# Stacked score operands built by the compute engines instead of by transfers, and products with v moved from five to seven tiles behind their scores

## The chip, the cores and the metric

The kernel runs on one core of a Trainium2 chip. A core has five engines with a queue each, which run their instructions in order: TensorE (PE; its weight loads are listed as PEld), VectorE (DVE), ScalarE (ACT), GpSimd (POOL) and SyncE (SP), which here only starts transfers. Sixteen DMA engines carry the transfers. SBUF is the memory on the core, with 128 partitions; PSUM takes TensorE's results. The metric is the time of one execution on the device in microseconds, as the median of several runs.

## The reference

Four batches of eight attention heads, 768 positions, 64 features a head; then a gating network of 512 model features and 1024 hidden features. Keys and queries are hashed to six bits each, and a query attends to the keys of its own bucket only:

```python
q_bits = (np.einsum('bhsd,dk->bhsk', q, proj) > 0).astype(np.int64)
k_bits = (np.einsum('bhsd,dk->bhsk', k, proj) > 0).astype(np.int64)
q_bucket = np.sum(q_bits * powers, axis=-1)
k_bucket = np.sum(k_bits * powers, axis=-1)
mask = q_bucket[:, :, :, None] == k_bucket[:, :, None, :]
scores = np.where(mask, scale * np.matmul(q, k.transpose(0, 1, 3, 2)), -1000000000.0)
scores = scores - np.max(scores, axis=-1, keepdims=True)
attn = np.exp(scores)
attn = attn / (np.sum(attn, axis=-1, keepdims=True) + 1e-09)
return np.matmul(attn, v).astype(np.float32)

h = np.maximum(x @ w_in, 0.0)      # x: the heads side by side
u, v = (h[..., :d_ff // 2], h[..., d_ff // 2:])
v_n = (v - mu) / np.sqrt(var + 1e-06)
v_s = np.einsum('ts,bsd->btd', w_spatial, v_n) + b_spatial[None, :, None]
gated = u * v_s
return (gated @ w_out).astype(np.float32)
```

## The kernel before, in words

The 32 heads are taken in 16 pairs, one pair on 128 partitions (64 features of each of two heads). Everything is computed in halves of 16 bits: a value is a rounded f16 (the high half) plus an f16 remainder (the low half).

*Loading and splitting a pair.* `load_qk` fetches k and q of a pair. `hash_rows` multiplies them with the projection on TensorE and makes the signs, `sg`, on VectorE: four strips of 32 partitions, one for each half of the 768 positions of k and of q (L178), then scaled in a second instruction (L180). `split_qk` makes the tile `hl` with four planes of 768: plane 1 and 2 are the high halves of k and q (ScalarE, L186), plane 0 and 3 the low halves of q and of k (VectorE, L187 and L188).

*Stacking a head.* `build(n)` fills one of four tiles `ab` of 128 x 4 x 768. Two matmuls per half then give a tile of scores with mask: one over 128 partitions, which adds high by low and low by high, and one that adds high by high and the hash codes, which stand under the 64 features and push a pair of different buckets far down. `build` works with transfers: the codes by four small ones per head (`ab<-sg`, L203), the low halves by a large one (`ab<-hl`, L216 or L217), and for the heads 8 to 31 (`near`) the upper planes by two copies on VectorE (L209, L210). For odd heads from 8 on the stack is upside down, so that the copies stay on their partitions. The small transfers start from SP's queue for heads 0 to 7 and from ScalarE's queue for the rest. `build(n + 2)` runs while head n is worked on.

*Scores.* Heads 1 to 7 (`KEYS`) are worked key-major: `row_max` first finds the maxima, then `scores_k` gives exponentials that are used as weights of `weighted_k` without a transpose. Head 0 and heads 8 to 31 are query-major, six tiles of 128 queries each: `scores` does two times two matmuls (L300, L301) into one of two PSUM tiles, VectorE evicts them with the row maximum (L302), ScalarE makes the exponential (L304) and its high half (L307), VectorE or GpSimd the low half (L308), and SP starts a transpose of both halves (L310, `pt<-pp`, 128 x 1536 f16). `weighted` multiplies the transposed tile with v in 18 matmuls (L323 to L325). There are six buffers for `pt`, four for `pp` and four for `ex`.

*The gating network.* After every eighth head 28 units of it are queued and mixed between the tiles: `vps` (L372), `ups` (L413), `sps` (L428), `ops` (L443). Those of the last batch have nothing left to be mixed with.

*What sets the order.* The loop at the end of the kernel runs over g, the number of a tile; `at(g, k)` gives the instructions a priority, and a scheduler fixes each engine's order when the program is built. `weighted` of tile t is emitted at step t + `LAG`, `LAG` being 5. `tc.issue_after(x)` keeps instructions behind x in their engine's order.

## Time and profile before

| what | value |
|---|---|
| median of 3 runs | 709.54 us (708.9 to 712.29) |
| the profiled execution | 708.95 us |
| its span, first to last instruction | 707.2 us |
| granted TensorE clock, mean | 0.964 |
| busy: TensorE, VectorE, ScalarE, GpSimd | 618.5, 511.3, 454.2, 222.0 us |
| TensorE's weight loads | 391.0 us |
| transfers: of SP's and ScalarE's queues | 109.67 MB, 77.0% of 16 engines' span |
| `pt<-pp` transposes, `ab<-hl`, `ab<-sg` | 150, 41, 128 transfers |

Busy shares are means over stretches that differ: a start in which the first operands are made, the key-major heads, the query-major heads with the gating network between them, and an end with the gating network alone. In rows of waits the engine that waits stands first and what ended its wait behind the arrow. In rows of groups the shape of the result stands ahead of `<-`, then the count, the busy time, the mean of one in ns, and the idle time before them. The clock is a share of full speed.

### The profile page before, as it was taken

How to read it: one execution, taken by the hardware profiler on the slowest of the kernel's cores; microseconds unless marked ns; L12 is line 12 of the kernel's file. 1: busy time of each engine (PE TensorE's matmuls, PEld its weight loads, DVE VectorE, ACT ScalarE, POOL GpSimd, SP SyncE). 2: the span in 40 equal slices, each digit the busy share in tenths (PEclk: the TensorE clock that was granted, in tenths of full speed). 3: DMA queues.
4: the chain of work that ended last, by engine and by line, in shares of the span. 5: the costliest groups of instructions: out<-in, count | busy, mean ns of one | idle time of the engine just before them, and what ended most of it. 6: DMA issues, size and time to landing. Idle time of an engine off the chain costs nothing.

```text
span 707.2 us, 14858 instructions
## 1 busy us (share of the span) xinstructions
PE 618.5 (87%) x5735; PEld 391.0 (55%) x5735; DVE 511.3 (72%) x961; ACT 454.2 (64%) x806; POOL 222.0 (31%) x215
## 2 busy tenths in 40 slices
PE   1668798999796989999796999899888999999997
PEld 0236676778453655565454565565445655655553
DVE  4665698388888897779699897899697987725100
ACT  1444477567686868777588786868677688724121
POOL 5111434454324452152002162033022530322513
PEclk9999798699899999999998999999999999999999
DMA  9557557353698979998989999999989899950011
GB/s 242 143 109 185 125 154 161 89 163 106 134 185 176 184 161 199 217 194 192 206 153 214 165 197 191 201 185 215 214 171 151 158 180 206 156 132 1 0 45 45
DMA packets 286555, 111.51 MB, mean 158 GB/s; under 512 B 270356, under 2 KB 273428, under 8 KB 286484
## 3 DMA queue, kind: packets, MB, share of 16 engines
q1 hardware_dynamic: 284180, 109.67, 77.0%
q10 hardware_dynamic: 2304, 0.89, 0.6%
q8 instruction: 45, 0.74, 0.4%
q14 instruction: 26, 0.21, 0.1%
HBM read 28.33 MB, written 6.29 MB: 49 GB/s over the span
## 4 chain that ended last, share of the span: by engine, by line
PE 48%; DMA 22%; DVE 11%; issue 7%; SPq 4%; ACT 4%; POOL 4%; ACTq 0%; DVEq 0%; POOLq 0%
DMA pt<-pp 14%; PE sps L428 7%; PE ops L443 7%; PE vps L372 6%; PE ups L413 6%; PE pv L282 4%; DMA ab<-hl 4%; PE sp L300 3%; PE sp L301 3%; PE pv L323 3%; SPq L310 2%; PE pv L325 2%; PE pv L324 2%; DVE ex L302 2%; PE sp L269 1%
## 5 line engine op out<-in xcount | busy, mean ns | idle before, releaser
L302 DVE TENSOR_SCALAR_CACHE_REDUCE ex<-sp 128x768 f32<-128x768 f32 x150 | 141.8, 951 | 42.1 <-PE sp L301 39.7
L304 ACT ACTIVATE ex<-ex,nb 128x768 f32<-128x768 f32 x150 | 139.3, 932 | 7.4 <-ACT nb L303 4.5
L323 PE MATMUL pv<-vp,pt 128*128 128x65 f16 x900 | 105.7, 196 | 43.3 <-DMA pt<-pp 42.7
L307 ACT CAST pp<-ex 128x768 f16<-128x768 f32 x150 | 123.7, 826 | 10.5 <-DMA pt<-pp 5.2
L308 DVE TENSOR_TENSOR pp<-ex,pp 128x768 f16<-128x768 f32 x116 | 123.1, 1064 | 9.5 <-ACT pp L307 8.9
L308 POOL TENSOR_TENSOR pp<-ex,pp 128x768 f16<-128x768 f32 x34 | 57.9, 1702 | 218.0 <-ACT pp L307 175.3
L323 PEld LDWEIGHTS <-pt 128*128 128x128 f16 x900 | 85.5, 100 | 70.7 <-DMA pt<-pp 61.8
L300 PE MATMUL sp<-ab 128*128 128x384 f16 x300 | 102.1, 340 | 14.4 <-DMA ab<-hl 9.3
L324 PE MATMUL pv<-vp,pt 128*128 128x64 f16 x900 | 105.4, 196 | 0.0
L325 PE MATMUL pv<-vp,pt 128*128 128x65 f16 x900 | 104.8, 197 | 0.0
L301 PE MATMUL sp<-ab 127*128 127x384 f16 (+1 forms) x300 | 102.2, 341 | 0.6 <-DMA ab<-sg 0.6
L428 PE MATMUL sps<-ws,vn 128*128 128x384 f16 x576 | 100.7, 326 | 0.5 <-DVE sy L432 0.5
L324 PEld LDWEIGHTS <-pt 128*128 128x128 f16 x900 | 85.9, 99 | 10.7 <-issue 1.9
L325 PEld LDWEIGHTS <-pt 128*128 128x128 f16 x900 | 86.0, 99 | 2.3 <-issue 0.6
L428 PEld LDWEIGHTS <-vn 128*128 128x128 f16 x576 | 54.3, 98 | 35.1 <-issue 1.8
L282 PEld LDWEIGHTS pv<-vf,ex 128*128 128x128 f32 x504 | 69.2, 210 | 3.2 <-issue 1.0
L372 PE MATMUL vps<-wi,xt 128*128 128x512 f16 x288 | 67.4, 382 | 3.2 <-DMA xt<-xs 3.2
L413 PE MATMUL ups<-xt,wi 128*128 128x384 f16 x384 | 69.4, 333 | 0.0
L443 PE MATMUL ops<-wo,g 128*128 128x512 f16 x288 | 67.8, 379 | 1.0 <-ACT o L447 0.9
L282 PE MATMUL pv<-vf,ex 128*128 128x65 f32 x504 | 68.0, 289 | 0.0
L303 ACT ACTIVATE nb<-mx 128x1 f32<-128x1 f32 x150 | 29.3, 197 | 57.2 <-DVE ex L302 56.2
L433 POOL TENSOR_TENSOR sy<-sy,u 128x384 f32<-128x384 f32 x32 | 35.9, 1125 | 75.5 <-DVE sy L432 54.5
(91 smaller groups left out, 920.8 us busy)
## 6 DMA issues: line engine op xcount, KB each, us to landing
qk<-kq SPq DMA_DIRECT2D x16, 768.0 KB
ab<-hl SPq DMA_DIRECT2D x34, 192.0 KB
out<-o SPq DMA_DIRECT2D x24, 256.0 KB
v<-v SPq DMA_DIRECT2D x13, 384.0 KB
raw<-w_in SPq DMA_DIRECT2D x16, 256.0 KB
ab<-hl SPq DMA_DIRECT2D x7, 384.0 KB
pt<-pp SPq DMA_TRANSPOSE x150
raw<-w_sp SPq DMA_DIRECT2D x12, 192.0 KB
```

What stands on the lines that cost most here:

```text
L282: nc.tensor.matmul(acc[:, qi, :], lhsT=ex[:, qi * P:(qi + 1) * P], rhs=vf[p % 2][:, 2 * i + e, :], start=(i == 0 and qi == 0), stop=(i == ...
L300: nc.tensor.matmul(ps[:, c], lhsT=t[:, 0, qs], rhs=t[:, 1, cs], start=True, stop=False)
L301: nc.tensor.matmul(ps[:, c], lhsT=t[0:K, 3, qs], rhs=t[0:K, 2, cs], start=False, stop=True)
L302: nc.vector.tensor_scalar(ex, ps, -float(2 ** 28), None, op0=ALU.max, op1=ALU.max, accum_out=mx)
L304: st["ex", n, i] = nc.scalar.activation(ex, ex, AF.Exp, bias=nb, scale=ISQ).ins
L307: nc.scalar.copy(pp[:, 0], ex)
L308: (nc.gpsimd if i in (PL_POOL if n >= 2 * NH else PL_POOL1) else nc.vector).tensor_tensor(out=pp[:, 1], in0=ex, in1=pp[:, 0], op=ALU.subtract)
L323: nc.tensor.matmul(acc, lhsT=pt[:, c, :], rhs=vh, start=(i == 0 and c == 0), stop=False)
L324: nc.tensor.matmul(acc[:, 0:D], lhsT=pt[:, c, :], rhs=vl, start=False, stop=False)
L325: nc.tensor.matmul(acc, lhsT=pt[:, NT + c, :], rhs=vh, start=False, stop=(i == NT - 1 and c == NT - 1))
L428: nc.tensor.matmul(ps[:, :HS], lhsT=vn[gv][:, c, d * P:(d + 1) * P], rhs=ws[gw][:, c, hs], start=(k == 0), stop=(k == 3 * NT - 1))
L443: nc.tensor.matmul(ps, lhsT=gt[h][gg][:, c, j * P:(j + 1) * P], rhs=wo[gw][:, c, :], start=(k == 0), stop=(k == 3 * NF - 1))
```

## The change

All transfers of `build` go. `build(n)` returns four parts, each an instruction or a few on an engine:

- `codes`: for each of the four strips one instruction that multiplies `sg` of 32 partitions with a column of a mask `hm` and writes 32 x 384 under the features; two on ScalarE and two on VectorE (all four on ScalarE for head 0). The mask holds the scale where the strip belongs to this head and zero elsewhere, so that L180 goes too. It is made once at the start by GpSimd and two instructions on VectorE.
- `high`: a copy of 64 x 1536, on GpSimd for even heads and VectorE for odd ones (ScalarE for head 0).
- `low`: a copy of 64 x 1536 on VectorE.
- `cross`: a copy of 64 x 1536 to the lower partitions, on VectorE for even heads and GpSimd for odd ones.

All heads now have the features on top, the clears of L199 go, and the second matmul uses 127 partitions for every head. For heads 8 to 31 the four parts are issued in four steps instead of one. `LAG` becomes 7. The half-precision copy, the low half and the transpose of a tile leave `scores` and become `halves`, called one step of the loop later with the same priority as before. `split_v` and `load_v` move by a few steps to match, and the row maxima of head 1 are spread over the first four steps.

```diff
+    hm = const.tile([P, 2], F32, name="hm")
+    hw = const.tile([P, 2, 4], F32, name="hw")
+    nc.gpsimd.memset(hw, 1.0)
+    nc.gpsimd.affine_select(out=hw, in_=hw, compare_op=ALU.is_ge, fill=0.0, base=0,
+                            pattern=[[-16, 2], [-32, 4]], channel_multiplier=1)
...
-        s1 = wk.tile([P, HS], F16, tag="sg1", bufs=2, name=f"sg1_{p}")
-        nc.vector.tensor_scalar(s1, s0, hv[:, 1:2], None, op0=ALU.mult)
-        st["sg", p] = s1
+        st["sg", p] = s0
...
-        q_s, q_h = (BQ_S[n >= NH], BQ_H[n >= NH])
-        near = n >= NH
-        z = D - D * e if near else D
-        if near and e and n < NH + NAB:
-            nc.gpsimd.memset(t[0:D, 2:4, :], 0.0)
-        if n < 1:
-            nc.sync.dma_start(out=t[0:D, 2:4], in_=hl[r, 1:3])
-        for j in range(4):
-            q_s.dma_start(
-                out=t[z:z + 2 * NB, 3 - j // 2, (j % 2) * HS:(j % 2 + 1) * HS],
-                in_=sg[32 * j + 16 * e:32 * j + 16 * e + 2 * NB, :])
-        if n < 1:
-            q_h.dma_start(out=t[0:D, 0:2], in_=hl[r, 0:2])
-        elif near:
-            nc.vector.tensor_copy(t[r, 2:4], hl[r, 1:3])
-            nc.vector.tensor_copy(t[r, 0:2], hl[r, 0:2])
-        else:
-
-            top = hl[r, 0:2]
-            (ps, pn), (ss, sn), (es, en) = top.ap
-            src = replace(top, ap=[(ps, pn), (ss, 2), (ss, 2), (es, en)])
-            q_h.dma_start(out=t[0:D].rearrange("p (a b) s -> p a b s", b=2), in_=src)
-        q_h.dma_start(out=t[z:z + D, 0:2], in_=hl[r, 2:4])
+
+        def codes():
+            for j in range(4):
+                js, hs = slice(32 * j, 32 * j + 32), slice((j % 2) * HS, (j % 2 + 1) * HS)
+                to = t[D:D + 32, 3 - j // 2, hs]
+                if j < 2 or n == 0:
+                    st["code"] = nc.scalar.activation(to, sg[js], AF.Copy, scale=hm[js, e:e + 1]).ins
+                else:
+                    nc.vector.tensor_scalar(to, sg[js], hm[js, e:e + 1], None, op0=ALU.mult)
+
+        def high():
+            if n == 0:
+                nc.scalar.copy(t[0:D, 2:4], hl[r, 1:3])
+            else:
+                OWN[e].tensor_copy(t[0:D, 2:4], hl[r, 1:3])
+
+        def low():
+            nc.vector.tensor_copy(t[0:D, 0:2], hl[r, 0:2])
+
+        def cross():
+            eng = nc.vector if n == 0 else OWN[1 - e]
+            st["cross"] = eng.tensor_copy(t[D:P, 0:2], hl[r, 2:4]).ins
+
+        return [codes, high, low, cross]
+
+    OWN = (nc.gpsimd, nc.vector)
...
-        K = P if n % 2 and n >= NH else P - 1
+        K = P - 1
...
-        at(NT * n + i + G_H, 50)
+        st["e32", n, i] = ex
+
+    def halves(n, i):
+        ex = st.pop(("e32", n, i))
...
-    LAG = 5
+    LAG = 7
+    SPL = 1
...
-            if i == BI and n + 2 < N:
-                build(n + 2)
+            if i == 0 and n + 2 < N:
+                parts = build(n + 2)
+            for part in parts[:1] if n + 2 >= NH else parts:
+                part()
+                parts = parts[1:]
...
+        if 0 <= g - SPL < N * NT and (g - SPL) // NT not in KEYS:
+            at(g - SPL + G_H, 50)
+            halves(*divmod(g - SPL, NT))
```

How the change moves instructions is seen at three places. In the rows a tile's own number stands ahead of the number of its buffer.

TensorE, where the products of tile 0 of head 21 begin (`ab_83` before and `ab_88` now are head 21, `ab_89` is head 22; the middle number of `sp_` and `pt_` is the tile). Before:

```order
L300 MATMUL sp_5_5594<-ab_83 128x384
L301 LDWEIGHTS ab_83
L301 MATMUL sp_5_5594<-ab_83 128x384
L323 LDWEIGHTS pt_0_5368
L323 MATMUL pv_5609<-vp_94,pt_0_5368 128x65
```

and now:

```order
L308 MATMUL sp_1_5611<-ab_89 128x384
L309 LDWEIGHTS ab_89
L309 MATMUL sp_1_5611<-ab_89 128x384
L334 LDWEIGHTS pt_0_5335
L334 MATMUL pv_5625<-vp_99,pt_0_5335 128x65
```

Before, the last scores ahead of the first product were those of tile 5 of the same head, five tiles on; now they are those of tile 1 of the next head, seven tiles on. Behind the last product with v of head 31 stand 18 matmuls of the third batch's network before, and 54 now.

VectorE, where the heads 26 and 27 (pair 13) are stacked while head 23's tiles are evicted. Before:

```order
L187 SCALAR_TENSOR_TENSOR hl_6063<-qk_5607,hl_6063 128x768
L188 SCALAR_TENSOR_TENSOR hl_6063<-qk_5607,hl_6063 128x768
L209 COPY ab_84<-hl_6063 64x1536
L209 COPY ab_85<-hl_6063 64x1536
L332 RECIPROCAL rv_6141<-rv_6141 128x6
L210 COPY ab_84<-hl_6063 64x1536
L210 COPY ab_85<-hl_6063 64x1536
```

and now:

```order
L192 SCALAR_TENSOR_TENSOR hl_5977<-qk_5508,hl_5977 128x768
L193 SCALAR_TENSOR_TENSOR hl_5977<-qk_5508,hl_5977 128x768
L208 TENSOR_SCALAR ab_90<-sg_13_5940,hm 32x384
L310 TENSOR_SCALAR ex_5_6060,mx_5817<-sp_5_6061 128x768
L208 TENSOR_SCALAR ab_90<-sg_13_5940,hm 32x384
L214 COPY ab_90<-hl_5977 64x1536
L319 TENSOR_TENSOR pp_3_6037<-ex_3_5967,pp_3_6037 128x768
L217 COPY ab_89<-hl_5977 64x1536
L217 COPY ab_90<-hl_5977 64x1536
L221 COPY ab_89<-hl_5977 64x1536
```

The four copies stay four; two of VectorE's four code writes of the pair come between (the other two stand a few rows earlier), and an eviction and a subtraction now stand among them.

ScalarE at the start of the program. Before:

```order
L186 ACTIVATE hl_121<-qk_110 128x1536
L223 ACTIVATE vp_94<-v_0_140 128x12x64
L186 ACTIVATE hl_167<-qk_132 128x1536
L303 ACTIVATE nb_142<-mx_143 128x1
L304 ACTIVATE ex_0_144<-ex_0_144,nb_142 128x768
```

and now:

```order
L191 ACTIVATE hl_126<-qk_115 128x1536
L212 COPY ab_87<-hl_126 64x1536
L206 ACTIVATE ab_87<-sg_0_124,hm 32x384 x4
L206 ACTIVATE ab_88<-sg_0_124,hm 32x384 x2
L231 ACTIVATE vp_99<-v_0_137 128x12x64
L311 ACTIVATE nb_148<-mx_149 128x1
L312 ACTIVATE ex_0_150<-ex_0_150,nb_148 128x768
```

The stacking of head 0 and half the codes of head 1 stand ahead of the first exponential, and the split of the second pair comes behind it.

More of the change, by code (lines that the diff above doesn't have):

```diff
@@ L176, in hash_rows @@
                 start=True, stop=True, tile_position=(0, 32 * j))
[L177 removed]
+        s0 = wk.tile([P, HS], F16, tag="sg0", bufs=2, name=f"sg0_{p}")
         nc.vector.tensor_scalar(s0, hp[:, :HS], 0.0, hv[:, 0:1], op0=ALU.is_gt, op1=ALU.subtract)
[L179 to L181 removed]
+        st["sg", p] = s0
     def split_qk(p):
@@ L501, in lsh_attention_spatial_gating @@
     load_qk(0)
+    nc.vector.reduce_sum(hm, hw, axis=AX.X)
+    nc.vector.tensor_scalar(hm, hm, hv[:, 1:2], None, op0=ALU.mult)
     hash_rows(0)
+    at(-40, 1)
     split_qk(0)
-    build(0)
-    load_qk(1)
-    build(1)
-    load_v(0)
+    at(-39, 0)
+    for part in build(0):
+        part()
+    load_v(0)
+    at(-38, 0)
+    load_qk(1)
+    at(0, 150)
+    first = st["cross"], st["code"]
+    with tc.issue_after(first[0]), tc.issue_after(first[1]):
+        for part in build(1):
+            part()
     at(-1, 0)
@@ L513, in lsh_attention_spatial_gating @@
     wv = 0
-    rml = [(NT * n + i - NT - LEAD, n, i) for n in sorted(KEYS) for i in range(NT)]
+    rml = [((0, 1, 2, 2, 3, 3)[i] if n == 1 else NT * n + i - NT - LEAD, n, i) for n in sorted(KEYS) for i in range(NT)]
     for g in range(N * NT + LAG):
@@ L524, in lsh_attention_spatial_gating @@
                 split_qk(1)
-                split_v(0)
+                with tc.issue_after(first[0]), tc.issue_after(first[1]):
+                    split_v(0)
                 load_qk(2)
@@ L534, in lsh_attention_spatial_gating @@
             stack = ExitStack()
-            if n not in KEYS:
+            if n not in KEYS and 'tr' in st:
                 stack.enter_context(tc.issue_after(st["tr"]))
-            if BQ_S[n + 2 >= NH] is nc.scalar or BQ_H[n + 2 >= NH] is nc.scalar:
+            if n + 2 >= NH:
                 stack.enter_context(tc.issue_after(st["ex", n, i]))
-            if i == BI and n + 2 < N:
-                build(n + 2)
+            if i == 0 and n + 2 < N:
+                parts = build(n + 2)
+            for part in parts[:1] if n + 2 >= NH else parts:
+                part()
+                parts = parts[1:]
             if n % 2 == 0:
```

12 lines of the change are left out of this document (6 added, 6 removed).

## The prediction

> **What bounds the kernel now.** I read the page first, then the span by stretches, then the chain and the waits of the longest stretch, then single groups and a stretch of the timeline. The page's span and its chain of waits by engine:
>
> ```profile
> span 707.2 us, 14858 instructions
> PE 48%; DMA 22%; DVE 11%; issue 7%; SPq 4%; ACT 4%; POOL 4%; ACTq 0%; DVEq 0%; POOLq 0%
> ```
>
> The execution took 708.95 us, of which 707.2 are the span; the median of the three runs shown is 709.54, 0.6 more. The chain is half TensorE, a fifth DMA. By stretches (the columns after the bounds are length, busy us of PE, PEld, DVE, ACT and POOL, granted clock, DMA share, GB/s):
>
> ```profile
> core 0: us, PE busy (x) PEld busy (x) DVE busy (x) ACT busy (x) POOL busy (x), PEclk, DMA share, GB/s
> 0.00:40.00 40.00, 16.97 (x69) 6.29 (x69) 21.32 (x29) 12.38 (x15) 13.61 (x25) 1.00 0.80 191
> 40.00:80.00 40.00, 27.74 (x247) 20.18 (x248) 27.03 (x54) 19.28 (x36) 7.67 (x10) 0.99 0.65 154
> 80.00:180.00 100.00, 96.27 (x661) 77.42 (x660) 75.52 (x155) 64.78 (x128) 45.01 (x59) 0.87 0.47 127
> 180.00:625.00 445.00, 400.16 (x4332) 246.47 (x4331) 372.23 (x688) 336.97 (x589) 133.72 (x100) 0.97 0.99 185
> 625.00:707.00 82.00, 77.39 (x431) 40.64 (x429) 15.18 (x38) 20.80 (x42) 22.00 (x22) 1.00 0.10 34
> ```
>
> The last 82 us are the gating network of the last batch, TensorE alone; nothing there is touched. From 80 to 180 us TensorE is busy 96 of 100. The stretch from 180 to 625 is where the query-major heads 8 to 31 run: TensorE 400 of 445, VectorE 372, ScalarE 337, DMA share 0.99. Nobody is full, so a loop of waits must set the pace. Its chain and its waits:
>
> ```profile
> by line: DMA pt<-pp 20.9%; issue 7.6%; PE ops L443 6.4%; PE sps L428 5.9%; PE ups L413 5.9%; PE vps L372 5.5%; PE sp L300 5.0%; PE sp L301 4.8%; PE pv L323 3.9%; DMA ab<-hl 3.5%; PE pv L325 3.2%; PE pv L324 3.1%; SPq L310 2.9%; DVE ex L302
> ACT nb L303 <- DVE ex L302: 40.3, 37, 3.8
> DVE ex L302 <- PE sp L301: 37.8, 33, 3.4
> PE pv L323 <- DMA pt<-pp: 36.6, 32, 3.2
> PEld L323 <- DMA pt<-pp: 53.6, 47, 3.6
> SPq L310 <- PE pv L325: 54.9, 40, 3.2
> ```
>
> The transposes lead the chain with 20.9% (93 us). TensorE waits 36.6 us for them at the first product with v of a tile; VectorE then waits 37.8 us for scores that stand behind that product in TensorE's order, and ScalarE 40.3 us for VectorE. The three numbers are one stall, passed on.
>
> **The change part by part.**
>
> *A, the distance of seven.* Products now stand seven tiles behind their scores instead of five (rows of TensorE ahead). A tile takes about 445/143 = 3.1 us here, so a transpose gets some 6 us more before it is asked for. I take all of the 36.6 us away from TensorE; bounds: nothing, and 53.6 us (the wait of the weight load, which contains it). What comes late next is VectorE, so the gain is counted there. Its idle time in the stretch is 445 - 372.2 = 72.8 us; without the 37.8 behind scores, 35 us stay.
>
> *B, VectorE's and GpSimd's new work in that stretch.* The rows:
>
> ```profile
> L180 DVE TENSOR_SCALAR sg<-sg,hc 128x384 f16<-128x384 f16 x10 | 6.8, 684 | 0.1
> L180 DVE TENSOR_SCALAR sg<-sg,hc x16: 301/318/1781, 11.1 to 546.4; 128x384 f16<-128x384 f16 x16
> L209 DVE COPY ab<-hl x24: 540/554/1420, 127.6 to 551.0; 64x1536 f16<-64x1536 f16 x24
> L85 DVE MEMSET ab<- 64x768 uint32 x2 | 1.4, 698 | 1.1 <-PEq L618 1.0
> L86 DVE MEMSET ab<- 32x768 f16 x2 | 1.4, 698 | 0.3 <-DVE ab L85 0.2
> L85 POOL MEMSET ab<- 64x1536 f16 x2 | 2.7, 1376 | 0.1
> L308 POOL TENSOR_TENSOR pp<-ex,pp x34: 1634/1647/2453, 26.7 to 612.5; 128x768 f16<-128x768 f32 x34
> ```
>
> Per pair of heads VectorE had four copies of 64x1536 and the second scaling of the codes (L180); now it has four copies of that shape again (one high, two low, one cross) and four code writes of 32x384, and GpSimd has two copies. A clear of 64 partitions and one of 32 both took 698 ns, so a code write of 32x384 is priced like L180's 128x384: median 318 ns. That is 4 x 0.318 - 0.318 = 0.95 us a pair, 9.5 us over the ten pairs of the stretch. With the stretch's mean of 684 ns, which holds waits, it is 20.5. I take 10, because the waits are priced apart: GpSimd. A GpSimd copy of 64x1536 is not in the trace; below it stands the clear of that size, 1.38 us, above it two of L308's subtractions of 768 elements, 2 x 1.65 = 3.3 us. Twenty copies are 28 to 66 us on an engine that is busy 134 of 445, so GpSimd itself bears them. What they cost VectorE:
>
> ```profile
> L308 DVE TENSOR_TENSOR pp<-ex,pp x116: 916/954/2398, 33.2 to 619.8; 128x768 f16<-128x768 f32 x116
> L308 DVE TENSOR_TENSOR pp<-ex,pp 128x768 f16<-128x768 f32 x112 | 118.7, 1062 | 8.3 <-ACT pp L307 7.7
> L302 DVE TENSOR_SCALAR_CACHE_REDUCE ex<-sp x150: 910/952/960, 23.6 to 615.9; 128x768 f32<-128x768 f32 x150
> 549.90 5.36 POOL L401 TENSOR_TENSOR vn<-vr,vn 128x512 f16<-128x512 f32 x3 [5.71 <-ACT vn L400]
> 550.44 1.98 DVE L209 COPY ab<-hl 64x1536 f16<-64x1536 f16 x2
> 552.45 1.80 DVE L308 TENSOR_TENSOR pp<-ex,pp 128x768 f16<-128x768 f32 x1
> ```
>
> Next to GpSimd's three operations the two copies took 1.98 us instead of 1.11 and a pair of operands out of SBUF 1.80 instead of 0.95, while the eviction from PSUM never passes 0.96. L308 loses (1062 - 954) x 112 = 12 us and L180 (684 - 318) x 10 = 4 us to 134 us of GpSimd, 0.12 us per us; for 28 to 66 us of copies that is 3 to 8 us, at most all 66. I take 4. Together VectorE has 372 + 14 busy and 35 idle: 421 instead of 445, a gain of **24 us**.
>
> *ScalarE* gets two code writes a head. The nearest row is a cast of 128x384:
>
> ```profile
> L434 ACT CAST g<-sy 128x384 f16<-128x384 f32 x32 | 16.3, 509 | 38.9 <-POOL sy L433 37.4 <-DMA ab<-sg 1.4
> L203 ACTq DMA_DIRECT2D ab<-sg x96: 727/736/1569, 149.9 to 574.1; - x96
> L217 SPq DMA_DIRECT2D ab<-hl x32: 462/865/1644, 10.0 to 578.9; - x32
> ```
>
> 20 heads x 2 x 0.51 = 20 us on an engine that is busy 337 of 445 and idles 40 of it behind VectorE; hidden there, and 20 us if that cover went. In exchange ScalarE's queue loses 96 issues of 0.74 us, SP's the issue of 0.87 us that stood between transposes once a head. The four clears of GpSimd and the two table instructions that make the masks run while the first load is under way. The removed bytes, (192 + 36) KB a head or 4.6 MB of the stretch's 185 GB/s x 445 us = 82 MB, also make room for the transposes. No separate gain is booked.
>
> *C, the start.* The first heads were stacked by transfers alone:
>
> ```profile
> 5.61 1.48 ACT L186 ACTIVATE hl<-qk 128x1536 f16<-128x1536 f32 x1 [3.60 <-DMA qk<-kq]
> 8.57 1.20 DVE L188 SCALAR_TENSOR_TENSOR hl<-qk,hl 128x768 f16<-128x768 f32 x1
> 16.49 0.50 PE L300 MATMUL sp<-ab 128*128 128x384 f16 x1 [9.27 <-DMA ab<-hl]
> 20.60 0.48 PE L301 MATMUL sp<-ab 127*128 127x384 f16 x1 [0.61 <-DMA ab<-sg]
> 23.62 0.95 DVE L302 TENSOR_SCALAR_CACHE_REDUCE ex<-sp 128x768 f32<-128x768 f32 x1
> ```
>
> q and k are split at 9.8 us, the scores begin whole only at 20.60. Now VectorE does the codes (0.61) and two copies (2 x 0.55) after 9.8 and is done at 11.5; ScalarE writes four codes of 0.5 after 10.4 and is done at 12.4. That is 8 us earlier. Head 1's stacking and the second pair's split now stand in VectorE's order between the first evictions, so I book **-7** (0 to -10).
>
> *D, to 180 us.* Pairs 1 to 3 now cost VectorE four copies and the codes: 4 x 0.55 + 0.95 = 3.2 us each, pairs 4 and 5 0.95, together 11.4 us in 140 us of which it was busy 103. TensorE sets that stretch (96 of 100): **+2** (0 to +11).
>
> *E, the end.* In TensorE's new order 54 matmuls of the third batch's network stand behind the last product with v, before 18.
>
> ```profile
> 418.02 5.85 PE sps L428 x36
> ```
>
> 36 of them took 5.85 us. They cost that if TensorE does not set the stretch before, nothing if it does; **+3**.
>
> Sum: 708.95 - 24 - 7 + 2 + 3 = 683 in the profile's own time, 683.5 as a median of runs: **683**.
>
> **The rivals.**
>
> *R1, the six buffers hold.* Only six transposed tiles fit, so the transpose of tile t must wait for the products of tile t - 6, which now stand a tile later than the scores of t. SP already waits 54.9 us, 40 times, for exactly that release. Against it: from that release to its own product a tile still has five others, about 15 us, and the longest single piece of a transpose on the chain is
>
> ```profile
> 406.45 6.69 DMA pt<-pp
> ```
>
> If half the stall stays, VectorE idles 35 + 19 = 54: 372 + 14 + 54 = 440, a gain of 5; 708.95 - 5 - 2 + 0.6 = **703**.
>
> *R2, slower: GpSimd's copies stop VectorE.* Each new copy runs where VectorE is to start one of its own. If each costs VectorE 2.3 us (the middle of 1.38 and 3.3), 20 are 46: 372 + 10 + 46 + 35 = 463, 18 more than now; with the other terms 708.95 + 18 - 2 + 0.6 = **726**. It decides once a copy costs more than (37.8 - 10)/20 = 1.4 us. The trace has 0.12 us per us, against it; the 550 us rows, where single instructions lose 0.85, are for it. The Trainium skill (SBUF — State Buffer, "Who interferes with whom") says that a VectorE instruction in a two-port mode or with two inputs in SBUF and a GpSimd instruction exclude one another for the whole instruction, whoever issued first; the rows at 550 us and the steady 0.96 us of the PSUM eviction agree with it. By that rule taken at its worst the time would be the 726 above; the mean of 0.12 says that most instructions miss each other.
>
> *R3, more is gained.* If the idle 35 us halve as well, 372 + 14 + 18 = 404, just above TensorE's 400: -41, and the time is 708.95 - 41 - 2 + 0.6 = **666**. For it: the 40 us of ScalarE's wait have the same root.
>
> That the DMA engines were the bound (share 0.99) would hardly move the time from the forecast: 4.6 of 82 MB is 5.5% of 445, 25 us. The change would then work by its bytes, not by its distance, and only experiments tell the two apart.
>
> **How the numbers follow.** The forecast has 0.58 (its own range 672 to 695, from VectorE's 9.5 to 20.5 us and the bounds of C, D and E), R1 0.17, R2 0.13, R3 0.12. The range reaches into R3 and over R1 to where R2 begins: 660 to 712. A measurement of this kernel tells about 0.5%, 3.5 us, from no change. Faster: 0.58 + 0.12 + 0.10 of R1 = 0.80; the rest of R1 is no change, 0.07; R2 0.13.
>
> **What would show it.** Right: in the stretch of the query-major heads TensorE's wait for transposes under 10 us instead of 36.6, VectorE's wait for scores under 15, VectorE busy 93% or so; first eviction near 13 us; 32x384 code writes near 0.3 us. R1: SP's wait for the products above 100 us and TensorE's wait still near 18. R2: L308's successor on VectorE well above 1.06 us on the mean, copies above 1 us. R3: VectorE above 95%. Wrong altogether: a code write or a GpSimd copy several times dearer than its nearest row, or TensorE's clock granted well below 0.97 there.

## The result, and the profile after

The changed kernel takes **742.1 us** (median of four executions, three of which took 739.48 to 742.69) against 709.56 of the kernel before beside it: a ratio of 1.0439, 95% interval 1.0395 to 1.0483. It is slower by 31 us by the ratio and 33 by the medians, where 683 was forecast and 712 was the upper end of the range. The fourth execution took 1027.49 us at about half the TensorE clock from end to end; the medians here and below count such slow executions, the ratios and intervals do not. The profile shown here is of another execution of the same kernel, 739.81 us. A second series of the same kernel gave 740.62 us, ratio 1.0476 (1.0408 to 1.0544).

The page of the changed kernel, span and busy time of the engines:

```profile
span 737.8 us, 14773 instructions
PE 626.9 (85%) x5735; PEld 396.7 (54%) x5735; DVE 589.8 (80%) x1025; ACT 493.7 (67%) x873; POOL 282.9 (38%) x247
```

VectorE was busy 511.3 us before and is now busy 78.5 us longer. By stretches, cut at 180 us and near the end of the query-major heads (625 us before and 655 now):

```profile
core 0: us, PE busy (x) PEld busy (x) DVE busy (x) ACT busy (x) POOL busy (x), PEclk, DMA share, GB/s
0.00:40.00 40.00, 16.04 (x109) 6.90 (x110) 34.91 (x48) 21.78 (x29) 19.64 (x30) 0.87 0.54 138
40.00:80.00 40.00, 34.26 (x224) 25.18 (x224) 32.58 (x61) 21.63 (x39) 12.98 (x17) 0.73 0.43 113
80.00:180.00 100.00, 89.15 (x661) 69.69 (x660) 79.69 (x149) 65.22 (x124) 48.59 (x56) 0.96 0.35 103
180.00:655.00 475.00, 409.95 (x4329) 254.47 (x4328) 428.73 (x736) 364.19 (x640) 177.86 (x124) 0.94 0.88 164
655.00:738.00 83.00, 77.53 (x417) 40.42 (x414) 13.86 (x34) 20.89 (x42) 23.84 (x24) 1.00 0.10 33
```

The loss lies in one row: the query-major stretch takes 475 us instead of 445, 30 of the 30.6 us by which the span grew. These cuts are times, and the two programs are not quite at the same place there. Cut by the program instead, the part from the first eviction of head 8 to the last product with v takes 478.6 us instead of 449.3, 29.3 more; head 8 begins 5.8 us earlier (172.48 us against 178.26), and what stands behind the last product takes 7.1 us longer (86.72 us against 79.62). In the long stretch VectorE is now the busiest engine, 428.7 us instead of 372.2, and the granted clock is 0.94 instead of 0.97. Its waits:

```profile
ACT nb L311 <- DVE ex L310: 74.9, 38, 7.3
PE sp L308 <- DVE ex L310: 40.3, 23, 3.9
PEld L334 <- DMA pt<-pp: 17.6, 16, 3.7
PE pv L334 <- DMA pt<-pp: 13.1, 13, 3.2
DVE ex L310 <- PE sp L309: 7.0, 10, 2.6
```

The direction of the stall has turned round. TensorE's wait for transposes fell from 36.6 to 13.1 us and VectorE's wait for scores from 37.8 to 7.0, as step A said. But TensorE now waits 40.3 us until VectorE has evicted a score tile, and ScalarE 74.9 us for VectorE (40.3 before). VectorE is late. Before, TensorE's wait for an eviction in the stretch was:

```profile
PE sp L300 <- DVE ex L302: 3.8, 7, 0.9
```

Why it is late is in the groups of instructions by shape (mean of one in ns behind the busy time):

```profile
L319 DVE TENSOR_TENSOR pp<-ex,pp 128x768 f16<-128x768 f32 x116 | 123.6, 1069 | 18.5 <-ACT pp L318 18.0
L208 DVE TENSOR_SCALAR ab<-sg,hm 32x384 f16<-32x384 f16 x62 | 34.4, 556 | 4.4 <-PE sp L278 2.6 <-PE sp L309 0.3
L217 DVE COPY ab<-hl 64x1536 f16<-64x1536 f16 x32 | 28.8, 901 | 1.0 <-PE sp L308 0.6
L193 DVE SCALAR_TENSOR_TENSOR hl<-qk,hl 128x768 f16<-128x768 f32 x16 | 28.3, 1768 | 0.0
L214 POOL COPY ab<-hl 64x1536 f16<-64x1536 f16 x15 | 26.1, 1740 | 57.5 <-ACT hl L191 52.2 <-PE sp L278 3.1 <-PE sp L309 2.2
L221 POOL COPY ab<-hl 64x1536 f16<-64x1536 f16 x16 | 26.0, 1628 | 26.0 <-DVE hl L193 17.4 <-PE sp L277 4.4 <-DVE rv L343 2.9
L206 ACT ACTIVATE ab<-sg,hm 32x384 f16<-32x384 f16 x66 | 40.4, 612 | 4.6 <-DVE sg L185 3.0 <-PE sp L278 0.3
```

and in the durations of one line (min/median/max in ns):

```profile
L208 DVE TENSOR_SCALAR ab<-sg,hm x62: 309/318/3104, 14.3 to 572.1; 32x384 f16<-32x384 f16 x62
L193 DVE SCALAR_TENSOR_TENSOR hl<-qk,hl x16: 945/1078/3822, 8.6 to 573.4; 128x768 f16<-128x768 f32 x16
L214 POOL COPY ab<-hl x15: 1456/1486/2248, 18.6 to 569.5; 64x1536 f16<-64x1536 f16 x15
L310 DVE TENSOR_SCALAR_CACHE_REDUCE ex<-sp x150: 911/950/959, 15.0 to 640.8; 128x768 f32<-128x768 f32 x150
```

The medians of the new instructions on VectorE and GpSimd are the prices that were forecast: 318 ns for a code write, and 1.49 us for a GpSimd copy, inside its bounds of 1.38 and 3.3. The means are not. A code write takes 556 ns on the mean and 3.1 us at worst, the copy of the low halves (L217) 901 instead of 555, the low half of k (L193) 1768, where the same line of the kernel before had 1098:

```profile
L188 DVE SCALAR_TENSOR_TENSOR hl<-qk,hl 128x768 f16<-128x768 f32 x16 | 17.6, 1098 | 0.0
```

Only instructions whose operands are all in SBUF have such tails in this trace; the eviction out of PSUM (L310) never passes 0.96 us. And the 116 subtractions of L319, which the prediction had named as the place to look, are as they were (1069 ns, before 1064). The losers are those which run while a pair is being stacked. The timeline of such a moment (start us, duration us):

```profile
490.51 1.10 DVE L192 SCALAR_TENSOR_TENSOR hl<-qk,hl 128x768 f16<-128x768 f32 x1
490.75 2.19 POOL L214 COPY ab<-hl 64x1536 f16<-64x1536 f16 x1
491.54 3.81 DVE L193 SCALAR_TENSOR_TENSOR hl<-qk,hl 128x768 f16<-128x768 f32 x1
492.90 1.63 POOL L319 TENSOR_TENSOR pp<-ex,pp 128x768 f16<-128x768 f32 x1
```

GpSimd's copy starts when ScalarE has made the high halves, and this is when VectorE makes the low halves of the same pair. VectorE's L193, at best 0.95 us, stood 3.81 us: GpSimd's copy ran until 492.94, its next instruction until 494.53, and VectorE ended 0.82 us after that.

How much that comes to: at their medians the new work of the whole span is 62 code writes x 0.318 = 19.7 us, less 16 scalings x 0.318 = 5.1, and 16 more copies x 0.555 = 8.9; together 23.5 us. VectorE's busy time grew by 78.5. The other **55 us** are instructions that took longer than at their medians, beyond those that already did before.

### The profile page after: what moved, and what is told of

The parts are those of the page before. It is cut to its first block, busy times and chain, and to the rows that moved or that the text cites. A ratio compares the mean times of both kernels' runs of the same rounds, so it can differ in the third digit from the quotient of the medians.

```text
span 1025.4 us, 14773 instructions
## 1 busy us (share of the span) xinstructions
PE 990.9 (97%) x5735; PEld 546.3 (53%) x5735; DVE 584.5 (57%) x1025; ACT 500.8 (49%) x873; POOL 277.1 (27%) x247
## 4 chain that ended last, share of the span: by engine, by line
PE 93%; DVE 4%; issue 1%; ACT 1%; DMA 1%; SPq 0%; DVEq 0%
PE sps L439 16%; PE ups L424 11%; PE vps L383 11%; PE ops L454 10%; PE pv L290 9%; PE sp L309 8%; PE sp L308 8%; PE pv L336 4%; PE pv L335 4%; PE pv L334 4%; PE sp L277 2%; PE sp L278 2%; PE mp L256 2%; PE hp L180 2%; DVE ex L310 1%
## 5 line engine op out<-in xcount | busy, mean ns | idle before, releaser
L310 DVE TENSOR_SCALAR_CACHE_REDUCE ex<-sp 128x768 f32<-128x768 f32 x150 | 142.9, 954 | 146.2 <-PE sp L309 140.2
L439 PE MATMUL sps<-ws,vn 128*128 128x384 f16 x576 | 172.3, 485 | 0.0
L308 PE MATMUL sp<-ab 128*128 128x384 f16 x300 | 143.1, 477 | 13.2 <-DVE ab L221 5.9
L334 PE MATMUL pv<-vp,pt 128*128 128x65 f16 x900 | 151.9, 232 | 0.5 <-DMA pt<-pp 0.4
L336 PE MATMUL pv<-vp,pt 128*128 128x65 f16 x900 | 150.5, 233 | 0.0
L335 PE MATMUL pv<-vp,pt 128*128 128x64 f16 x900 | 148.9, 231 | 0.0
L309 PE MATMUL sp<-ab 127*128 127x384 f16 x300 | 145.3, 484 | 0.0
L319 DVE TENSOR_TENSOR pp<-ex,pp 128x768 f16<-128x768 f32 x116 | 121.1, 1047 | 6.6 <-ACT pp L318 6.1
L334 PEld LDWEIGHTS <-pt 128*128 128x128 f16 x900 | 107.7, 122 | 28.8 <-issue 26.5
L335 PEld LDWEIGHTS <-pt 128*128 128x128 f16 x900 | 106.4, 120 | 27.8 <-issue 27.6
L319 POOL TENSOR_TENSOR pp<-ex,pp 128x768 f16<-128x768 f32 x34 | 60.4, 1778 | 220.7 <-ACT pp L318 182.7
L454 PE MATMUL ops<-wo,g 128*128 128x512 f16 x288 | 116.7, 578 | 0.8 <-ACT o L458 0.8
L424 PE MATMUL ups<-xt,wi 128*128 128x384 f16 x384 | 115.4, 484 | 0.0
L383 PE MATMUL vps<-wi,xt 128*128 128x512 f16 x288 | 115.1, 580 | 0.0
L336 PEld LDWEIGHTS <-pt 128*128 128x128 f16 x900 | 103.7, 117 | 9.5 <-issue 9.3
L290 PEld LDWEIGHTS pv<-vf,ex 128*128 128x128 f32 x504 | 100.5, 289 | 8.9 <-issue 6.3
```

The costliest lines, as they stand in the source:

```text
L290: nc.tensor.matmul(acc[:, qi, :], lhsT=ex[:, qi * P:(qi + 1) * P], rhs=vf[p % 2][:, 2 * i + e, :], start=(i == 0 and qi == 0), stop=(i == ...
L308: nc.tensor.matmul(ps[:, c], lhsT=t[:, 0, qs], rhs=t[:, 1, cs], start=True, stop=False)
L309: nc.tensor.matmul(ps[:, c], lhsT=t[0:K, 3, qs], rhs=t[0:K, 2, cs], start=False, stop=True)
L310: nc.vector.tensor_scalar(ex, ps, -float(2 ** 28), None, op0=ALU.max, op1=ALU.max, accum_out=mx)
L319: (nc.gpsimd if i in (PL_POOL if n >= 2 * NH else PL_POOL1) else nc.vector).tensor_tensor(out=pp[:, 1], in0=ex, in1=pp[:, 0], op=ALU.subtract)
L334: nc.tensor.matmul(acc, lhsT=pt[:, c, :], rhs=vh, start=(i == 0 and c == 0), stop=False)
```

## The experiments

Each time is the median of a series, with the kernel before timed beside it. Span, busy time and clock are those of one profiled execution, which need not be the median one; none is used for the copies on ScalarE.

| kernel | us | ratio to before (95%) | span | VectorE busy, whole span | clock |
|---|---|---|---|---|---|
| the change | 740.62 | 1.0476 (1.0408 to 1.0544) | 737.8 | 589.8 | 0.933 |
| stacking alone | 743.18 | 1.0503 (1.0434 to 1.0572) | 740.3 | 584.7 | 0.940 |
| distance alone | 693.27 | 0.9792 (0.9727 to 0.9858) | 689.6 | 517.3 | 0.973 |
| change, GpSimd's copies on VectorE | 698.10 | 0.9870 (0.9793 to 0.9947) | 694.6 | 563.6 | 0.960 |
| change, GpSimd's copies on ScalarE | 696.53 | 0.9837 (0.9770 to 0.9905) | | | |
| that on VectorE, with idle copies on GpSimd | 734.06 | 1.0357 (1.0280 to 1.0433) | 730.6 | 593.8 | 0.939 |
| change, large copies partly by transfers | 698.97 | 0.9878 (0.9814 to 0.9941) | 700.2 | 541.8 | 0.968 |
| distance of six | 693.20 | 0.9760 (0.9695 to 0.9825) | 692.1 | 518.0 | 0.962 |
| distance of seven, five input buffers | 691.24 | 0.9776 (0.9740 to 0.9813) | 688.6 | 515.6 | 0.982 |
| the same, seven transposed tiles | 696.08 | 0.9839 (0.9798 to 0.9879) | 698.8 | 514.8 | 0.954 |
| distance, first pair stacked by engines | 687.71 | 0.9724 (0.9668 to 0.9779) | 686.4 | 529.5 | 0.957 |
| the same, codes of three heads moved | 691.55 | 0.9715 (0.9636 to 0.9794) | 681.0 | 530.1 | 0.967 |

### The two halves of the change, apart

The change was run again beside its two halves.

> The change once more, for a profile and an interval on this chip. Theory 1 (clock): TensorE is granted a lower clock than before (about 0.935 against 0.964 on the mean) in a few stretches, and the time lost lies in these; TensorE's waits for transposes are below 10 us in the query-major stretch. Theory 2 (VectorE): the clock is as before and VectorE is busy above 93% there, its two-input operations well above 1.06 us. Theory 3 (buffers): TensorE still waits 30 us or more for transposes, and SP waits above 100 us for products. Time 738 to 746 in all three.

*The stacking alone* keeps the engine stacking and the new start, and puts the distance and the products' preparation back:

```diff
-    LAG = 7
-    SPL = 1
+    LAG = 5
...
+        at(NT * n + i + G_H, 50)
+        halves(n, i)
...
-        if 0 <= g - SPL < N * NT and (g - SPL) // NT not in KEYS:
-            at(g - SPL + G_H, 50)
-            halves(*divmod(g - SPL, NT))
```

> The stacking by engines and the new start alone; products five tiles behind, the half-precision copy, low half and transpose where they were. Theory 2 (VectorE and GpSimd exclude each other): nearly all of the loss is here, 730 to 745 us. Theory 3 (buffers): 690 to 705 us, since the stacking is not what costs. Theory 1 (clock): near the kernel before or a little faster, 695 to 710, with the clock at 0.96.

*The distance alone* is the kernel before with seven tiles, the late halves and the moved `split_v` and `load_v`; operands are stacked by transfers:

```diff
-    LAG = 5
+    LAG = 7
+    SPL = 1
...
+        if 0 <= g - SPL < N * NT and (g - SPL) // NT not in KEYS:
+            at(g - SPL + G_H, 50)
+            halves(*divmod(g - SPL, NT))
```

> The distance of seven and the later copy and transpose alone (with the loads and the split of v that go with it); the stacking by transfers and the start as before. Theory 3 (buffers): 730 us or more, TensorE still waiting for transposes. Theory 2: 685 to 700, the waits gone and VectorE with no new work. Theory 1 (clock): the waits gone, a denser TensorE and a clock below 0.95; 700 to 725.

The stacking alone costs 36 us (743.18 against 707.31) and the distance alone gains 14 (693.27 against the same 707.31). They don't add: both together should have cost 22 and cost 33. Next to the stacking the distance is worth 2.6 us, and the intervals overlap, so it may be nothing. One profile of each, cut at the same places of the program (in us; the stretch runs from the first eviction of head 8 to the last product with v), shows where this comes from:

| kernel | up to head 8 | stretch | VectorE busy, idle in it | behind it |
|---|---|---|---|---|
| before | 178.3 | 449.3 | 373.9, 75.4 | 79.6 |
| distance alone | 167.8 | 435.1 | 379.6, 55.5 | 86.6 |
| stacking alone | 170.5 | 489.8 | 426.5, 63.4 | 80.0 |
| the change | 172.5 | 478.6 | 432.9, 45.7 | 86.7 |
| change, GpSimd's copies on VectorE | 163.7 | 444.2 | 403.8, 40.5 | 86.7 |

In the stretch the distance takes away 14.2 us alone and 11.2 beside the stacking, so there the two nearly add. At the end it costs some 7 us in both cases (step E). What fails to add lies ahead of head 8: the distance reaches it 10.4 us earlier than before, the stacking 7.8, and both together 5.8. Why stays open; single executions differ there, and the three profiles with a distance of seven and stacking by transfers alone reach head 8 at 167.8, 169.2 and 175.4 us.

The distance alone, in the query-major stretch and in its waits over the whole span:

```profile
180.00:605.00 425.00, 388.32 (x4294) 242.85 (x4293) 369.52 (x676) 327.69 (x575) 132.20 (x96) 0.98 1.03 191
```

```profile
PEld L326 <- DMA pt<-pp: 31.8, 30, 2.4
PE pv L326 <- DMA pt<-pp: 22.7, 26, 2.0
```

Between these cuts the stretch is 20 us shorter than before with nearly the same VectorE work (369.5 us), and VectorE idles 55.5 us instead of 72.8. TensorE still waits 22.7 us for transposes, where it waited 42.7 before. With the stacking alone TensorE waits for them as well as for VectorE, in the rows of the whole span:

```profile
PE pv L336 <- DMA pt<-pp: 31.1, 23, 3.8
PE sp L308 <- DVE ex L310: 29.7, 26, 3.7
```

In the change, over the whole span, the first of these waits is 14.3 us and the second 45.3: TensorE waits for VectorE instead.

### Is it GpSimd's copies?

Thirty-one copies of 64x1536 run on GpSimd. If they stop VectorE (R2's mechanism), giving VectorE *more* work by moving them there must make the kernel faster; if VectorE simply has too much to do, it must get slower.

```diff
-    OWN = (nc.gpsimd, nc.vector)
+    OWN = (nc.vector, nc.vector)
```

> The change, with GpSimd's 31 copies given to VectorE. Theory L (exclusion): GpSimd's copies of 1.5 us hold up VectorE's two-input instructions and copies; without them the mean of a code write on VectorE falls from 0.56 us to 0.35, of the second low half of a pair from 1.77 to 1.1, and the kernel is faster than the change although VectorE carries 31 x 0.555 = 17 us more: 705 to 725 us. Theory W (work): it is VectorE's own number of instructions that costs; 750 to 760 us.

It took 698.10 us, 44 less than the change's 742.1 and 42.5 less than its second series. VectorE took over 31 x 0.555 = 17 us of copies, and yet its busy time *fell* by 26. Its query-major stretch and three groups:

```profile
180.00:610.00 430.00, 389.73 (x4261) 244.37 (x4260) 390.01 (x717) 349.51 (x610) 137.04 (x94) 0.96 0.95 175
```

```profile
L214 DVE COPY ab<-hl 64x1536 f16<-64x1536 f16 x31 | 24.2, 781 | 0.3
L208 DVE TENSOR_SCALAR ab<-sg,hm 32x384 f16<-32x384 f16 x62 | 23.7, 383 | 2.4 <-PE sp L278 0.7 <-PE sp L309 0.4
L193 DVE SCALAR_TENSOR_TENSOR hl<-qk,hl 128x768 f16<-128x768 f32 x16 | 21.3, 1330 | 0.0
```

A code write is down to 383 ns on the mean, L193 to 1330, and the stretch to 430 us. What VectorE is busy beyond its work at medians fell from 55.0 us to 563.6 - 511.3 - 23.5 - 17.2 = 11.6. The difference, 43.4 us, is about the whole difference in time.

The same copies on ScalarE:

```diff
-    OWN = (nc.gpsimd, nc.vector)
+    OWN = (nc.scalar.copy, nc.vector.tensor_copy)
```

> The change, with GpSimd's 31 copies given to ScalarE. Theory L: VectorE's means fall as above with no work added to it; 700 to 715 us. Theory W: VectorE's own code writes and copies stay, so little changes; 730 to 745. Theory Q (ScalarE's place): 31 copies of some 1.5 us between exponentials delay the tiles; 745 or more.

696.53 us. Of the three engines that were tried for these copies, only GpSimd cost the time.

The opposite test adds GpSimd copies that nothing needs to the kernel with all stacking on VectorE. At each of the 31 places where GpSimd had copied, it copies the same source in three pieces into a tile that is never read:

```diff
+    scr = const.tile([D, 512], F16, name="scr")
...
+    def idle(src):
+        flat = src.rearrange("p a s -> p (a s)")
+        for k in range(3):
+            nc.gpsimd.tensor_copy(scr, flat[:, 512 * k:512 * k + 512])
```

> The run with all copies on VectorE (698 us), and beside it on GpSimd, at the same places of the program, three copies of 64x512 into a spare tile that nothing reads, for each copy that the change gave to GpSimd (93 small copies, about 50 us of GpSimd). No result waits for them. Theory L (exclusion): they alone hold VectorE up, its two-input instructions and copies rise again; 715 to 745 us. Theory D (lateness: GpSimd's copies were late parts of the stacked operand, for which the scores waited): no more than 698 to 704.

734.06 us, 36 more than without them. The copies, the low half of k beside them, and the stretch of the query-major heads:

```profile
L235 POOL COPY scr<-hl 64x512 f16<-64x512 f16 x93 | 80.4, 864 | 39.2 <-ACT hl L192 32.2 <-DVE rs L416 2.5 <-DVE hl L194 0.9
```

```profile
L194 DVE SCALAR_TENSOR_TENSOR hl<-qk,hl 128x768 f16<-128x768 f32 x16 | 30.5, 1907 | 0.0
```

```profile
180.00:646.00 466.00, 406.05 (x4312) 250.85 (x4311) 422.94 (x741) 356.03 (x626) 191.86 (x159) 0.94 0.89 164
```

VectorE has the same instructions as in the kernel without the idle copies and is busy 593.8 us instead of 563.6: 30.2 us of lengthening, for a loss of 36. So the loss is not that GpSimd delivers the operands late, since nothing takes these. A part may be GpSimd's queue: SP stood 15.3 us behind these copies, because GpSimd's own low halves queue behind them. In the change this part is small: SP waits 9.7 us for GpSimd's low halves there, and 8.4 where VectorE does the stacking.

### Is it the code writes?

Here only the codes are written by engines. The large copies are those of the kernel before: VectorE's two for the heads from 8 on, and transfers for the rest (head 0 stays on engines).

```diff
+            elif n >= NH:
+                nc.vector.tensor_copy(t[0:D, 2:4], hl[r, 1:3])
             else:
-                OWN[e].tensor_copy(t[0:D, 2:4], hl[r, 1:3])
+                nc.sync.dma_start(out=t[0:D].rearrange("p (a b) s -> p a b s", b=2), in_=src)
...
-            eng = nc.vector if n == 0 else OWN[1 - e]
-            st["cross"] = eng.tensor_copy(t[D:P, 0:2], hl[r, 2:4]).ins
+                nc.sync.dma_start(out=t[D:P, 0:2], in_=hl[r, 2:4])
```

> Of the stacking by engines only the hash codes are kept (and head 0); the large parts are made as before, with high and low copied by VectorE for heads 8 to 31 and the cross part by a transfer of 192 KB. Distance of seven. Theory L: no copy of GpSimd is left, VectorE has 40 code writes of 0.32 us more than in the run of the distance alone (693 us); 695 to 705. Theory W: the code writes are the cost; 715 to 730.

698.97 us, against 693.27 for the distance alone: the ratios to before, 0.9878 and 0.9792, have overlapping intervals. The code writes cost some 6 us or nothing, and are not where the 47 us went by which the change stands above the distance alone.

### Why the distance gained 14 us and not 38

R1 said that a transpose must wait for one of six buffers. If so, seven tiles of distance are worth no more than six, and a seventh buffer must help.

```diff
-    LAG = 7
+    LAG = 6
```

> The distance alone, six instead of seven. If the six buffers of transposed tiles make seven worth no more than six (rival R1), the time is that of seven, 691 to 696 us, and TensorE waits some 23 us for transposes as there. If the distance counts in full, 697 to 702, between five (708) and seven (693).

Six gave 693.20 us and seven 693.27; TensorE's wait for transposes is 25.4 us with six and 22.7 with seven. So far this is as R1 said. The seventh buffer finds room in memory only if the gating network's input has five buffers instead of six. Both were run, the second as the control:

```diff
-    PTB = 6
-    XTB = 6
+    PTB = 7
+    XTB = 5
```

> The kernel with the distance alone, with seven buffers for the transposed tiles instead of six; the memory for the seventh is taken from the buffers of the gating network's input, five instead of six. If six buffers are what halves the gain of the distance (R1), a transpose no longer waits for the product that stands behind the scores of its own tile: SP's wait for products (52.3 us with six) falls below 30, TensorE's wait for transposes (22.7) below 12, and the time is 5 to 12 us below the 693 of the distance alone, 681 to 688. If the transposes are late for another reason (SP's own order: 53.5 us behind VectorE's low halves, 25.4 behind scores), the time stays at 690 to 695 and the wait for transposes near 20.

> The control of the run with seven buffers: the distance alone, six buffers for the transposed tiles, and five instead of six for the gating network's input. Both theories: no change against the 693 of the distance alone, 690 to 697; if the fifth buffer is short, a few us more, and the run with seven has to be read against this one.

With seven buffers it took 696.08 us, the control 691.24. In the waits of the whole span, with seven buffers:

```profile
PE pv L326 <- DMA pt<-pp: 23.7, 25, 2.6
```

```profile
SPq L313 <- PE pv L328: 49.9, 38, 2.5
```

TensorE waits as long as with six (control 23.3), and SP stands behind products as long (control 47.9). The extra buffer at the same distance brings nothing back, so that R1 falls in the form that it had. Seven buffers at a distance of seven stand to each other as six do at six, and an eighth buffer was not tried, so a limit that moves along with the distance isn't excluded. What keeps TensorE waiting some 23 us for transposes at six and at seven stays open. The longest wait of their start on SP is for VectorE's low halves (53.8 us over the span with the distance alone, 71.1 with six); no run took it away. A run with a distance of five and late halves wasn't made either, so it isn't told apart how much of the 14 us comes from the distance and how much from the later halves.

### The start by itself

The distance alone, with only the first two heads stacked by engines and the new start:

```diff
-    build(0)
-    load_qk(1)
-    build(1)
+    for part in build(0):
+        part()
...
+    with tc.issue_after(first[0]), tc.issue_after(first[1]):
+        for part in build(1):
+            part()
```

> The distance of seven with the first pair alone stacked by engines, all other heads as before the change. If the start gains what the prediction said, 7 us below the run of the distance alone, 684 to 689; if the start's gain is given back by the key-major heads, 691 to 695.

In this kernel the operand of head 5 keeps 16 rows with codes of head 1 below its own, so that head 5's mask isn't the reference's; the instructions are as many and as long. It took 687.71 us. In the next kernel the codes of heads 3, 5 and 7 stand 16 rows lower, over those rows:

```diff
-                    z = D - D * e if n >= NH else D
+                    z = D - D * e if n >= NH else D + 16 * e
```

> The distance of seven with the first pair alone stacked by engines, the codes of heads 3, 5 and 7 sixteen rows lower so that they cover those of head 1. Same instructions on the engines as the run before it (687.7 us): 685 to 690, which would be the fastest kernel here.

691.55 us, a little above the 685 to 690 expected, ratio 0.9715 (0.9636 to 0.9794); the distance alone had 0.9792 (0.9727 to 0.9858). The start seems to gain up to 6 us when GpSimd takes no large part in it, but the intervals overlap, and it is not shown. Every kernel here in which GpSimd makes at most one of the large copies is faster than the kernel before; by the ratios these two are the fastest.

## Why the prediction was wrong

| step | forecast | measured |
|---|---|---|
| A, TensorE's wait for transposes in the stretch | from 36.6 to under 10 us | 13.1 |
| A, VectorE's wait for scores | from 37.8 to under 15 | 7.0 |
| A alone, on the time | 38, before VectorE's new work | 14 |
| B, VectorE busy in the stretch | 386 us | 428.7 |
| B, VectorE idle in the stretch | 35 us | 46.3 |
| C, first whole scores | 12.4 us | 13.56 |
| C and D, start of head 8 | -5 | -5.8 |
| C and D, VectorE busy up to head 8 | 11.4 more | 18.8 more |
| E, the end | +3 | +7.1 |

The stretch of A and B is between the cuts of the forecast here. Cut by the program, the 57 us between the sum of 683 and the profile's 739.8 are these: in the stretch VectorE's busy time grew by 59.0 us instead of 14, which is 45 us, and its idle time fell by 29.7 instead of 37.8, which is 8; the end is 4 us longer than booked, and the start came within a microsecond.

**A** was right in kind and too large. The stall goes, as the waits say, but the idle time that it held is not all handed back: alone, by the places of the program, it shortens the stretch by 14 us, and VectorE's idle time by 20 of the 37.8 that were counted. This is nearly R1's size (half the stall, idle 54 us; measured 55.5), though its reason, the six buffers, was not borne out. Its own sign was missing too: SP's wait for products in the stretch should have passed 100 us and is shorter than the 54.9 before,

```profile
SPq L321 <- PE pv L336: 45.2, 39, 2.5
```

Beside the stacking A works as well: VectorE idles 45.7 us instead of 63.4 and the stretch is 11 us shorter. The time gains only 2.6 us from it, because the end takes 7 of them and head 8 begins 2 us later.

**B** is the step that failed, by one term: "*I take 4*" for what GpSimd's copies cost VectorE. The durations of single instructions were forecast well (code write 0.318 us, GpSimd copy 1.49, both medians). Over the whole span the lengthening is 55 us beside 52.1 us of GpSimd copies (26.1 + 26.0), 1.06 us per us, against the forecast's 0.12. Less the 11.6 us that are left with the copies on VectorE, it is 43.4 us: 0.83 us per us, or 1.4 us for each of the 31 copies. The price of 0.12 was a mean over all of GpSimd's work, and of VectorE's losses it counted two groups only, though others lost too (L209: a mean of 644 ns at a median of 554). Why the mean was so far off is likely, but no run moved the same copies to other moments to show it: the new copies are not spread. They are released by the same instructions as VectorE's low halves and copies of the pair, so they tend to run beside the instructions that they stop. The 550 us rows of the trace before showed such a case; the mean was preferred to them.

**R2** had the right mechanism. Its sum put VectorE at 372 + 10 + 46 = 428 us in the stretch, and the trace has 428.7. So close a match is luck in part. With the copies on VectorE instead, VectorE is busy 403.8 us in the stretch and not 432.9, though 20 x 0.555 = 11 us of copies came to it. That is 40 us of lengthening, 2.0 us a copy, and some 6 us of it are the splitting of weights (L144 to L147), which one kernel does in this stretch and the other ahead of it. So a copy costs 1.7 to 2.0 us there, below the 2.3 taken and above the 1.4 from which R2 was to decide. Two of its signs did not come: L319 is at 1.07 us, as L308 was, and the copies of L217 at 0.90 are below 1. Its time of 726 is too low by 16, because VectorE's idle time is 46.3 us and not 35, and the end costs 7 us and not 3. The rule cited there, Trainium skill, SBUF — State Buffer, "Who interferes with whom" (a shared port pair of VectorE and GpSimd that one of them holds alone), agrees with the runs: tails where both operands lie in SBUF, none for the eviction from PSUM, and none of the loss once GpSimd's copies are elsewhere. That the port is what stops VectorE is taken from that page; the runs show only who stops whom, and for how long.

**ScalarE's** code writes took 612 ns on the mean against 509 of the row taken (L206 in the groups above); the engine is busy 364 of 475 in the stretch, and they are hidden, as said. **C** came a microsecond later than worked out: the first whole scores (L309) at 13.56 us, and the first eviction, said to be near 13, at 14.99 instead of 23.62:

```profile
10.20 1.46 POOL L221 COPY ab<-hl 64x1536 f16<-64x1536 f16 x1
10.60 1.47 DVE L217 COPY ab<-hl 64x1536 f16<-64x1536 f16 x1
13.26 0.50 PE L308 MATMUL sp<-ab 128*128 128x384 f16 x1 [5.88 <-DVE ab L221]
13.56 0.53 PE L309 MATMUL sp<-ab 127*128 127x384 f16 x1
14.99 0.96 DVE L310 TENSOR_SCALAR_CACHE_REDUCE ex<-sp 128x768 f32<-128x768 f32 x1
```

The collision is there in the first operand already: VectorE's copy takes 1.47 us beside GpSimd's instead of 0.55. But eight us earlier at the first tile are not eight at head 8: VectorE has by then been busy 141.0 us instead of 122.2, 18.8 more (11.4 were booked under **D**), and head 8 begins 5.8 us earlier. C and D were booked with 5 us. That this matches is luck: the distance alone, without the new start, begins head 8 earlier still.

**E** was priced at 5.85 us for 36 matmuls, nothing if hidden, and booked with 3. It came in full and a little over: what stands behind the last product with v takes 86.7 us instead of 79.6. The range of 672 to 695 that the forecast gave itself does not follow from the bounds that it names either; added up, they reach from 674 to 712.

**The clock** was named as one of the things that would make the forecast wrong, and it is 0.94 in the stretch instead of 0.97. Three slices of 5 us of the changed kernel:

```profile
210.00:215.00 5.00, 1.39 (x22) 1.03 (x23) 5.00 (x12) 2.26 (x4) 0.00 (x0) 1.00 0.86 161
215.00:220.00 5.00, 2.29 (x7) 0.94 (x7) 5.00 (x11) 4.29 (x11) 2.64 (x2) 0.52 0.14 29
220.00:225.00 5.00, 3.92 (x48) 2.67 (x47) 5.00 (x13) 4.89 (x11) 1.41 (x2) 0.80 1.15 217
```

VectorE is full, TensorE gets 1.39 us of work in the first slice, and in the next its clock is halved. Of the 84 such slices from 180 to 600 us, 19 have a clock under 0.9 in the change, 17 with the idle copies, 9 with the copies on VectorE, 8 in the kernel before and 6 with the distance alone; ahead of the 19, TensorE was busy 3.2 us of 5 on the mean, ahead of the slices at full clock 4.5. The Trainium skill, TensorE: Matmul & The Clock Gate, "What's actually happening", says that a stretch without work halves the clock, and these rows agree. So a late VectorE can cost twice, once as a wait and once as a slower TensorE: from head 8 to the last product TensorE is busy 410.6 us for 4320 matmuls, and 393.7 for 4323 with the distance alone. How much of the loss is the second was not tested: no run kept TensorE's clock up while VectorE was late.

**The DMA engines** were not the bound in the sense of the prediction's last alternative: the share fell from 0.99 to 0.88 in the stretch, and the kernel that stacks on VectorE (0.95) is no faster than the one that keeps the transfers (1.03). The share of 1.03 at the fastest stretch leaves open that the transfers hold back what is left.

## What to carry to other kernels

Before work is moved to GpSimd, look at what releases it: if the same event releases VectorE's instructions on SBUF operands, reckon that VectorE may stand still for as long as GpSimd runs (0.8 to 1.1 us per us for the whole copies here, 0.4 for the idle pieces), and not by the mean over a trace. A mean far above the median in a group of VectorE's instructions, with a PSUM eviction that stays flat, is the sign to look for, and moving the copies back onto VectorE is a cheap test. A stall that was passed on by three engines was worth less here than its row showed; of 38 us only 14 to 20 came back. And compare stretches between the same instructions, not the same times: the distance seems worthless beside the stacking until the stretch, the start and the end are cut apart.

## What had not been expected of the hardware

- One VectorE instruction can stand behind two GpSimd instructions in turn: 3.81 us for an operation of 0.95.
- 31 GpSimd copies, 52 us of an engine that was busy 38% of the span, cost 42 to 44 us of the kernel's time; the kernel that gives these copies to VectorE, 17 us more of work for it, is the faster by that much.
- The same source copied in pieces of 512 to an idle tile lengthened VectorE's work by 30.2 us beside 80.4 us, 0.38 us per us. The 80.4 us hold lengthening of GpSimd's own: at their shortest, 0.60 us, the 93 pieces are 56 us. The price is not one of GpSimd's busy time alone.
- A seventh buffer for the transposed tiles changed no wait, though before the change SP stood behind products 40 times in the stretch, as if for a buffer.
